# Windowed attention ahead of two expert layers: the scores of a head pair's groups, moved from zero-padded full tiles to quarters of TensorE

## The chip, the core and the metric

The kernel runs on one core of one Trainium2 chip. The metric is the device time of one execution in microseconds (us), lower is better. The engines in the text: PE is TensorE (PEld its weight loads), ACT is ScalarE, DVE is VectorE, POOL is GpSimd, SP is SyncE, which here only starts DMAs.

## What is computed

Three stages follow each other. Attention: 4 batches, 8 heads, 576 positions, head size 64, each query sees the last 64 positions. Then a mixture of 8 experts, each token to one expert, then a dense layer with a clipped quadratic activation. All in fp32. The change touches attention and the way its result X is handed on:

```python
scores = scale * np.matmul(q, k.transpose(0, 1, 3, 2))
rel = pos[:, None] - pos[None, :]
scores = np.where((rel >= 0) & (rel < 64), scores, -1e9)
attn = softmax(scores)
x = np.matmul(attn, v)                     # (B, H, S, D)
x = x.transpose(0, 2, 1, 3).reshape(2304, 512)
logits = x @ w_gate + modality_bias[modality_id]   # argmax picks the expert
out[mask] = gate_w[mask] * (relu(x[mask] @ w1[e]) @ w2[e])
...
return g(out @ w_in) @ w_out
```

## The kernel before

The 2304 tokens are 36 groups of 64 queries, 9 groups to a batch. A group of queries meets 128 keys: the 64 before it and its own (the first group of a batch takes the first 128 keys and another mask). A loop over steps g = 0 to 39 is written as a software pipeline, and each engine runs its instructions in the order in which they are written. In step g:

- `scores(g + 1)`: four matmuls write the bank `sc`, one for each head pair hp. Heads are laid out as par = 0 or 1 on partitions 0 to 63 or 64 to 127, four hp each. The stationary operand is the query tile `Q[:, g, hp]`, 128 partitions by 128 columns, in which each head's 64 queries stand on its own 64 partitions and the rest is zero; so 128 rows of scores come out, 64 for each head of the pair. DVE scales and masks the bank into `sm` (L467) and reduces its maximum to `nm` (L470).
- `turn(g - 1)`: four transposes of the exponentials into `pt`. `weigh(g - 2)`: eight matmuls, each on 64 columns of the array, from `et` and the values V into `o`. In even steps `gates` transposes the X of two groups (one tile of 128 tokens) into `xp`. Every fourth step has the gate's `lp`, every fourth `L` (four small passes of 8 columns).
- On ACT `expo(g)`, four exponentials that take `nm` as bias and sum into `su`; `turned(g - 1)`, the copy of `pt` to `et`; in even steps `gated`, two copies of `xp` halves to `xt`.
- On DVE `norm(g - 1)` and `weighed(g - 2)`, which writes X; then two DMAs on SP store X of the group, one for each par, to `xs` in DRAM.

A block j of three groups is loaded by SP at the start of step 3(j - 2): `load_q` with two DMAs (one for each par, 256 bytes at a time into the zero-padded tile, of which there are three, cleared once by DVE), K with one, V with one. Blocks 0 and 1 are loaded in smaller pieces at the start. SP starts its DMAs strictly in program order, and each waits until the eighth before it has landed.

Behind attention run pieces of the routing (`route`): for each chunk of 4 tiles some 25 small DVE operations, spread over the steps by `between` and `advance`, with a store of `gate` to `xs` (L690). From about step 23 on SP also loads the first expert's eight weight pieces (L241), and POOL splits six of them into a high and a low part (L915, L916); between the third and the fourth POOL starts the gather of block 0's rows from `xs` (L256). Before step 32's scores stand 7 matmuls of `keep` that only pass time; the scores of group 33 behind them are the first that need block 11. PSUM has 7 banks in rotation for all of this.

Of the kernel before, what the change touches and what calls it, by code (L numbers as in the profile page):

```python
# [85 lines left out]
def moe_kernel(tc, qh, kh, vh, wgh, mod, mbias, wall, winh, wouth, out):  # L86
    nc = tc.nc
    with ExitStack() as ctx:
# [26 lines left out]
        mask = [kp.tile([P, P], F32, name=f"mask{i}") for i in range(2)]  # L115
        for i in range(2):
            nc.gpsimd.memset(mask[i], 0.0)
            for par in range(2):
                m = mask[i][par * 64:(par + 1) * 64, :]
                if i == 0:  # L120
# [283 lines left out]
        with tc.tile_pool(name="ap", bufs=2, side="right", reuse_waits="tile") as ap, tc.tile_pool(name="rp", bufs=2, side="right", reuse_waits="tile") as rp:  # L404
            NQ = 3
            qz = [ap.tile([P, 3, 4, 2, 64], F32, name=f"qz{i}", bufs=1) for i in range(NQ)]
            for i in range(NQ):
                for par in range(2):
                    nc.vector.memset(qz[i][64 * par:64 * par + 64, :, :, 1 - par], 0.0)
# [3 lines left out]
            def load(j, then=None):  # L413
# [45 lines left out]

            def scores(g):  # L460
                b, gi, s = win(g)
                Q, K = st["Q", g // 3], st["K", b]
                sc = bank("sc", (P, 4, P))
# [3 lines left out]
                nc.vector.scalar_tensor_tensor(out=sm, in0=sc, scalar=0.125, in1=mask[gi == 0].unsqueeze(1).to_broadcast([P, 4, P]), op0=ALU.mult, op1=ALU.add)  # L467
# [31 lines left out]
            def weigh(g):  # L499
                b, gi, s = win(g)  # L500
                V = st["V", b * 3 + s // 3]
                et = st.pop(("t", g))
                o = bank("o", (P, 4, 64))
# [6 lines left out]
            def weighed(g):  # L510
                o, rc = st.pop(("o", g)), st.pop(("r", g))
                if g % 2 == 0:
                    st["x", g // 2] = ap.tile([P, 2, 4, 64], F32, name="X", bufs=3)
                X = st["x", g // 2]
                nc.vector.tensor_mul(X[:, g % 2], o, rc.unsqueeze(2).to_broadcast([P, 4, 64]))
                for par in range(2):
                    sl = slice(par * 64, par * 64 + 64)
                    nc.sync.dma_start(xs[g * 64:g * 64 + 64, par * 256:par * 256 + 256], X[sl, g % 2].rearrange("p h d -> p (h d)"))

            def gates(t):  # L520
                X = st.pop(("x", t))
                xp = bank("xp", (P, 2, 2, 2, 64))
                for gi in range(2):
                    for i in range(2):
                        nc.tensor.transpose(xp[:, gi, i].rearrange("p a b -> p (a b)"), X[:, gi, 2 * i:2 * i + 2].rearrange("p a b -> p (a b)"), ident)
                st["xp", t] = xp

            def gated(t):
                xp = st.pop(("xp", t))
                if t % 2 == 0:  # L530
                    st["xt"] = ap.tile([P, 2, 2, 2, 2, 64], F32, name="xt", bufs=1)
                for gi in range(2):
                    nc.scalar.copy(st["xt"][:, :, :, t % 2, gi], xp[:, gi])

            def logits(t):
# [3 lines left out]
                for j in range(4):  # L539
                    nc.tensor.matmul(lp[32 * j:32 * j + 32], wgs[:, j], xt[:, j % 2, j // 2].rearrange("p t a b -> p (t a b)"), start=True, stop=True)  # L540
                st["lp"] = lp

            def logits1(t):
                st["lx"] = st["xt"][:, 0, 0].rearrange("p t a b -> p (t a b)")
# [1255 lines left out]
```

## Time and profile before

| | us |
|---|---|
| median of 3 runs (lowest, highest) | 802.19 (800.89, 805.43) |
| the profiled execution | 807.45 |
| its span in the profile | 805.7 |
| PE busy (share of the span) | 763.7 (95%) |
| PEld busy | 658.4 (82%) |
| DVE busy | 505.9 (63%) |
| ACT busy | 350.0 (43%) |
| POOL busy | 301.1 (37%) |

The shares are means over the whole span. Attention takes about the first 125 us of it, and there the shares are others; the rows below are from that stretch. "Clock" is the share of full speed that was granted to TensorE: 1.00 is 2.4 GHz, 0.50 is 1.2 GHz. An fp32 matmul shows as two passes, each with a weight load and a matmul, so four matmuls are eight such pairs.

### The profile page before, as it was taken

What the parts mean: (1) busy time and instruction counts of PE and PEld (TensorE: products, weight loads), DVE (VectorE), ACT (ScalarE), POOL (GpSimd) and SP (SyncE); (2) the same over time, 40 slices, a digit from 0 to 9 for tenths busy, and PEclk for the clock granted to TensorE, in tenths of its full rate; (3) what the DMA queues carried; (4) which work ended last, traced back from release to release, by engine and by line L of the source; (5) the groups of instructions that cost most, each with busy time, mean ns of one, the idle gap of its engine ahead of it and who ended that gap; (6) DMA issues with size and microseconds to landing.
All of it is one profiled execution on the core that took longest, in us unless ns stands there. A gap on an engine that the chain in (4) does not pass through costs nothing. (4 is left out here: it accounts for less than half of the span.)

```text
span 805.7 us, 14482 instructions
## 1 busy us (share of the span) xinstructions
PE 763.7 (95%) x4935; PEld 658.4 (82%) x4935; DVE 505.9 (63%) x1012; ACT 350.0 (43%) x827; POOL 301.1 (37%) x257
## 2 busy tenths in 40 slices
PE   6999979999999999989799899999989999999996
PEld 5888868999878886868697679999988888888874
DVE  6788886787766466511675556798868356453540
ACT  4899743232233324523353434344445435433440
POOL 5000572124323153201453332335625656475441
PEclk8999979999999999999899999999999999999999
DMA  8888941357887959445574565748845444353411
GB/s 204 236 224 259 287 149 33 112 194 244 287 282 280 314 197 360 150 148 170 147 235 156 183 211 164 214 156 267 281 173 150 120 135 117 104 143 107 130 46 39
DMA packets 101014, 149.21 MB, mean 185 GB/s; under 512 B 30096, under 2 KB 65456, under 8 KB 100928
## 3 DMA queue, kind: packets, MB, share of 16 engines
q1 hardware_dynamic: 95664, 132.30, 52.4%
q0 software_dynamic: 4736, 15.61, 6.2%
q8 instruction: 41, 0.67, 0.3%
q14 instruction: 45, 0.37, 0.1%
q10 hardware_dynamic: 528, 0.26, 0.1%
HBM read 132.00 MB, written 45.50 MB: 220 GB/s over the span
## 5 line engine op out<-in xcount | busy, mean ns | idle before, releaser
L1610 POOL TENSOR_TENSOR AR<-RA,AR 128x768 fp32r<-128x768 f32 x43 | 81.8, 1923 | 44.0 <-ACT AR L1609 43.9
L82 POOL TENSOR_TENSOR cv_g<-cv_g,cv_a 128x512 f32<-128x512 f32 x32 | 45.2, 1426 | 128.3 <-DVE cv_a L80 82.8
L1724 PE MATMUL ob<-WG,AR 128*128 128x512 f32 x234 | 91.9, 393 | 0.8 <-POOL AR L1610 0.4
L1722 PE MATMUL ob<-WG,AR 128*128 128x512 f32 x234 | 91.5, 391 | 0.0
L1723 PE MATMUL ob<-WG,AR 128*128 128x512 f32 x234 | 91.2, 390 | 0.0
L380 PE MATMUL hp<-xh,AR 128*128 128x256 f32 x512 | 71.1, 280 | 0.0
L380 PEld LDWEIGHTS hp<-xh,AR 128*128 128x128 f32 x512 | 64.6, 188 | 4.7 <-issue 3.4
L1601 DVE TENSOR_SCALAR small<-RA 128x768 f32<-128x768 f32 x48 | 43.7, 912 | 37.7 <-DMA RA<-gs 37.7
L1602 ACT ACTIVATE small<-small,half 128x768 f32<-128x768 f32 x48 | 45.0, 939 | 41.5 <-DVE small L1601 41.5
L477 ACT ACTIVATE ex<-sm,nm 128x128 f32<-128x128 f32 x144 | 56.1, 395 | 14.2 <-DVE nm L470 13.9
L1470 PE MATMUL mz<-AR,WG 128*128 128x384 f32 (+2 forms) x258 | 54.9, 348 | 6.8 <-ACT AR L1202 1.9
L1608 DVE TENSOR_TENSOR RA<-small,RA 128x768 f32<-128x768 f32 x48 | 56.0, 1166 | 7.2 <-ACT small L1602 6.0
L1470 PE MATMUL mv<-AR,WG 128*128 128x384 f32 (+2 forms) x258 | 54.8, 348 | 3.3 <-ACT wide L1510 2.2
L389 DVE SCALAR_TENSOR_TENSOR hl<-hp,hh 128x512 fp32r<-128x512 f32 x32 | 21.9, 690 | 57.2 <-ACT hh L388 35.3
L1470 PEld LDWEIGHTS mz<-AR,WG 128*128 128x128 f32 x258 | 46.3, 194 | 9.6 <-DVE small L1503 2.4
L1724 PEld LDWEIGHTS ob<-WG,AR 128*128 128x128 f32 x234 | 43.9, 188 | 12.3 <-POOL AR L1610 2.9
L1609 ACT CAST AR<-RA 128x768 fp32r<-128x768 f32 x48 | 39.9, 831 | 32.3 <-PE ob L1723 16.2
L398 PE MATMUL yp<-AR,hh 128*128 128x512 f32 x128 | 52.3, 409 | 0.6 <-ACTq L351 0.6
L1470 PE MATMUL mx<-AR,WG 128*128 128x384 f32 x252 | 51.5, 342 | 0.9 <-ACTq L1147 0.8
L1723 PEld LDWEIGHTS ob<-WG,AR 128*128 128x128 f32 x234 | 43.9, 188 | 9.5
L1722 PEld LDWEIGHTS ob<-WG,AR 128*128 128x128 f32 x234 | 44.0, 188 | 9.1
L400 PE MATMUL yp<-AR,hl 128*128 128x512 f32 x128 | 50.6, 395 | 0.0
(395 smaller groups left out, 1738.7 us busy)
## 6 DMA issues: line engine op xcount, KB each, us to landing
WR<-in_wall_dram SPq DMA_DIRECT2D x80, 256.0 KB
RA<-in_wall_dram SPq DMA_DIRECT2D x36, 512.0 KB
raw<-in_wall_dram SPq DMA_DIRECT2D x36, 512.0 KB
RA<-gs SPq DMA_DIRECT2D x48, 384.0 KB
gs<-small SPq DMA_DIRECT2D x51, 192.0 KB
cv_r<-in_winh_dram SPq DMA_DIRECT2D x16, 512.0 KB
gs<-wide SPq DMA_DIRECT2D x36, 192.0 KB
V<-in_vh_dram SPq DMA_DIRECT2D x7, 768.0 KB
```

Of the source, the lines that this page charges most:

```text
L82: nc.gpsimd.tensor_add(z, z, x)
L380: nc.tensor.matmul(o, a, c, start=n == 0, stop=n == 11)
L398: nc.tensor.matmul(yp, h, wh, start=f == 0, stop=False)
L400: nc.tensor.matmul(yp, l, wh, start=False, stop=f == 7)
L477: nc.scalar.activation(ex[:, hp], sm[:, hp], AF.Exp, bias=nm[:, hp:hp + 1], scale=1.0, accum_out=su[:, hp:hp + 1])
L1470: nc.tensor.matmul(out, a, b, start=first and n == 0, stop=n == 5, skip_group_check=not first or part is not ALLT)
L1602: nc.scalar.activation(GQ[n % 4], GQ[n % 4], AF.Square, scale=0.5, bias=half[:, 0:1])
L1608: nc.vector.tensor_max(GT[n % 5], GQ[n % 4], GT[n % 5])
L1610: eng.tensor_sub(l, GT[n % 5], h)
L1722: nc.tensor.matmul(obs[i], h[:, sl], wh, start=f == j == 0, stop=False)
L1723: nc.tensor.matmul(obs[i], h[:, sl], wl, start=False, stop=False)
L1724: nc.tensor.matmul(obs[i], l[:, sl], wh, start=False, stop=f == 7 and j == 1)
```

## The change

Two groups, 2t and 2t + 1, are now taken together. `products(t)` issues 16 matmuls: for each hp and each of the two groups and each par, 64 partitions of queries by 64 columns against 128 keys. Each uses one quarter of the array (its rows by par, its columns by group), and the two par write two banks. What was "the work of group g" in all later functions is now the work of par = g % 2 of both groups. Sizes and counts of `sm`, `nm`, the exponentials, `et` and `o` stay as they were. `products` is issued in the odd steps only, for two groups at once, so the scores of an odd group come one step earlier in PE's order than before.

Q is loaded without zeros: one DMA of 128 partitions for a block, and the six clears by DVE go. X of a tile is stored by one DMA of 128 tokens in place of four. `gated` is one copy in place of two. There are three masks (a third for a pair whose second group opens a batch). The first loads are cut otherwise: queries of groups 0 and 1 in one DMA, then V, K, queries of group 2.

```diff
-            qz = [ap.tile([P, 3, 4, 2, 64], F32, name=f"qz{i}", bufs=1) for i in range(NQ)]
-            for i in range(NQ):
-                for par in range(2):
-                    nc.vector.memset(qz[i][64 * par:64 * par + 64, :, :, 1 - par], 0.0)
+            qz = [ap.tile([P, 3, 4, 64], F32, name=f"qz{i}", bufs=1) for i in range(NQ)]
...
-                    for par in range(2):
-                        nc.sync.dma_start(Q[par * 64:par * 64 + 64, g0:g1, :, par],
-                                          qh[par * 64:par * 64 + 64, (3 * j + g0) * 256:(3 * j + g1) * 256].rearrange("p (g h q) -> p g h q", g=g1 - g0, h=4))
+                    nc.sync.dma_start(Q[:, g0:g1].rearrange("p g h q -> p (g h q)"), qh[:, (3 * j + g0) * 256:(3 * j + g1) * 256])
...
                     load_k(nc.scalar, 0, 128)
-                    load_q(0, 1)
-                    load_q(1, 3)
+                    load_q(0, 2)
+                    load_v(0, 1)
                     load_k(nc.sync, 128, 192)
-                    load_v(0, 1)
+                    load_q(2, 3)
...
+            def products(t):
+                sc = [bank("sc", (P, 4, P)) for par in range(2)]
+                for hp in range(4):
+                    for gi in range(2):
+                        g = 2 * t + gi
+                        b, _, s = win(g)
+                        for par in range(2):
+                            sl = slice(par * 64, par * 64 + 64)
+                            nc.tensor.matmul(sc[par][gi * 64:gi * 64 + 64, hp], st["Q", g // 3][sl, g % 3, hp], st["K", b][sl, hp, s * 64:s * 64 + 128], start=True, stop=True)
+                for par in range(2):
+                    st["sc", 2 * t + par] = sc[par]
+
             def scores(g):
-                for hp in range(4):
-                    nc.tensor.matmul(sc[:, hp], Q[:, gi % 3, hp].rearrange("p a b -> p (a b)"), K[:, hp, s * 64:s * 64 + 128], start=True, stop=True)
+                if g % 2 == 0:
+                    products(g // 2)
+                sc = st.pop(("sc", g))
...
                 for hp in range(4):
-                    for par in range(2):
+                    for gi in range(2):
...
                         nc.tensor.matmul(o[sl, hp], et[:, hp, sl], V[:, s % 3, hp * P + par * 64:hp * P + par * 64 + 64], start=True, stop=True)
...
-                for par in range(2):
-                    sl = slice(par * 64, par * 64 + 64)
-                    nc.sync.dma_start(xs[g * 64:g * 64 + 64, par * 256:par * 256 + 256], X[sl, g % 2].rearrange("p h d -> p (h d)"))
+                if par:
+                    nc.sync.dma_start(xs[t * P:t * P + P, 0:D], X.rearrange("p a h d -> p (a h d)"))
...
-                for gi in range(2):
-                    nc.scalar.copy(st["xt"][:, :, :, t % 2, gi], xp[:, gi])
+                nc.scalar.copy(st["xt"][:, :, t % 2], xp)
```

How the instructions stand now shows best on two engines. On PE, in the middle of attention, this is the order before (line, operation, tiles, size and count; `sc` are scores, `pt` the transposed exponentials, `o` the weighed values):

```order
L465 MATMUL sc<-K,qz_220 128x128 x4
L491 MATMUL pt<-ident,ex 128x128 x4
L507 MATMUL o<-V,et 64x64 x8
L465 MATMUL sc<-K,qz_220 128x128 x4
L491 MATMUL pt<-ident,ex 128x128 x4
L525 MATMUL xp<-ident,X 128x128 x4
L507 MATMUL o<-V,et 64x64 x8
```

And this is the same place of the changed kernel:

```order
L466 MATMUL sc<-K,qz_234 64x128 x16
L501 MATMUL pt<-ident,ex 128x128 x4
L518 MATMUL o<-V,et 64x64 x8
L501 MATMUL pt<-ident,ex 128x128 x4
L535 MATMUL xp<-ident,X 128x128 x4
L518 MATMUL o<-V,et 64x64 x8
```

Eight score matmuls in two batches of four have become sixteen smaller ones in one batch ahead of two steps' other work.

On SP, one block's loads and the X stores around them, before:

```order
L422 DMA qz_221<-in_qh_dram 64x12x64 x2
L426 DMA K<-in_kh_dram 128x4x192
L433 DMA V<-in_vh_dram 128x3x512
L518 DMA xs<-X 64x256 x6
L422 DMA qz_222<-in_qh_dram 64x12x64 x2
```

And in the changed kernel, two blocks long, since a tile's store falls now once, now twice to a block:

```order
L419 DMA qz_235<-in_qh_dram 128x768
L422 DMA K<-in_kh_dram 128x4x192
L429 DMA V<-in_vh_dram 128x3x512
L529 DMA xs<-X 128x512 x2
L419 DMA qz_236<-in_qh_dram 128x768
L422 DMA K<-in_kh_dram 128x4x192
L429 DMA V<-in_vh_dram 128x2x512
L699 DMA xs<-gate 128x4x16
L529 DMA xs<-X 128x512
```

Ten DMAs to a block have become four or five.

On PE around the 7 passing matmuls (`warm`), before; the scores that are the first to read block 11 stand right behind them:

```order
L465 MATMUL sc_1737<-K_1193,qz1_221 128x128 x4
L491 MATMUL pt_1747<-ident_76,ex_1652 128x128 x4
L540 MATMUL lp_1752<-xt_1634,wgs_103 32x256 x4
L507 MATMUL o_1757<-V_1194,et_1731 64x64 x8
...
L857 MATMUL warm_1798<-ident_76 128x128 x7
L465 MATMUL sc_1806<-K_1193,qz2_222 128x128 x4
```

And now, where the first matmul that reads block 11's queries (`qz2`) is the third row:

```order
L466 MATMUL sc_1801<-K_1240,qz1_235 64x128
L466 MATMUL sc_1802<-K_1240,qz1_235 64x128
L466 MATMUL sc_1801<-K_1240,qz2_236 64x128
...
L501 MATMUL pt_1824<-ident_76,ex_1725 128x128 x4
L549 MATMUL lp_1829<-xt_1695,wgs_117 32x256 x4
L518 MATMUL o_1834<-V_1241,et_1796 64x64 x8
...
L866 MATMUL warm_1874<-ident_76 128x128 x7
```

The first use of block 11 has moved from behind the passing matmuls to a place ahead of them, one step earlier.

## Rows read from the trace of the kernel before

**Rows 1.** Busy time by window: from:to, length, engines (instructions), clock, DMA share, GB/s.

```profile
16.00:21.60 5.60, 5.21 (x34) 4.79 (x35) 2.06 (x5) 2.23 (x9) 0.64 (x2) 0.50 1.03 224
24.00:80.00 56.00, 55.66 (x710) 48.42 (x709) 46.60 (x152) 51.50 (x218) 0.00 (x0) 1.00 0.86 238
...
106.40:112.20 5.80, 0.22 (x3) 0.00 (x1) 5.80 (x9) 2.12 (x9) 5.64 (x5) 0.84 0.28 99
112.20:123.40 11.20, 11.20 (x84) 8.89 (x85) 6.38 (x26) 6.26 (x19) 4.99 (x6) 0.50 0.36 89
```

**Rows 2.** Timeline of PE's weight loads, steps 7 to 11: start, length, instructions, [idle before].

```profile
30.26 0.55 PEld L507 LDWEIGHTS o<-V,et 128*64 128x64 f32 x16 [0.41 <-DVE sm L467]
30.87 0.97 PEld L465 LDWEIGHTS sc<-K,qz 128*128 128x128 f32 x8
31.76 0.47 PEld L491 LDWEIGHTS pt<-ident,ex 128*128 128x128 f32 x4
...
32.20 0.53 PEld L554 LDWEIGHTS L<-selg,xt 128*128 128x128 f32 x4
...
40.09 0.16 PEld L540 LDWEIGHTS lp<-xt,wgs 128*32 128x32 f32 x8 [0.17 <-ACT ex L477]
40.66 0.43 PEld L507 LDWEIGHTS o<-V,et 128*64 128x64 f32 x12 [0.41 <-issue]
```

**Rows 3.** Timeline of ACT, the copies of an even step.

```profile
38.05 0.56 ACT L496 COPY et<-pt 128x512 f32<-128x512 f32 x1
38.52 0.63 ACT L533 COPY xt<-xp 128x256 f32<-128x256 f32 x2
```

**Rows 4.** Waits of DVE, 24 to 80 us: total us, times, longest.

```profile
DVE sm L467 <- PE sc L465: 7.4, 16, 0.7
```

**Rows 5.** Timeline of the start: scores of group 4, and ACT around them.

```profile
11.11 0.56 ACT L496 COPY et<-pt 128x512 f32<-128x512 f32 x1
...
14.75 0.40 ACT L477 ACTIVATE ex<-sm,nm 128x128 f32<-128x128 f32 x1
...
16.39 2.04 PE L465 MATMUL sc<-K,qz 128*128 128x128 f32 x8 [3.52 <-DMA qz<-in_qh_dram]
...
19.92 0.40 ACT L477 ACTIVATE ex<-sm,nm 128x128 f32<-128x128 f32 x1
...
23.52 0.42 ACT L477 ACTIVATE ex<-sm,nm 128x128 f32<-128x128 f32 x1
```

**Rows 6.** Timeline of SP, which starts the DMAs: start, length of the issues.

```profile
65.84 3.73 SPq L518 DMA_DIRECT2D xs<-X  x6
70.32 1.34 SPq L422 DMA_DIRECT2D qz<-in_qh_dram  x2
...
72.45 0.45 SPq L433 DMA_DIRECT2D V<-in_vh_dram  x1
...
93.48 0.63 SPq L426 DMA_DIRECT2D K<-in_kh_dram  x1
```

**Rows 7.** Timeline of the end of attention, all engines.

```profile
73.91 0.40 ACT L477 ACTIVATE ex<-sm,nm 128x128 f32<-128x128 f32 x1
...
82.36 0.40 ACT L477 ACTIVATE ex<-sm,nm 128x128 f32<-128x128 f32 x1
...
93.64 0.97 PEld L465 LDWEIGHTS sc<-K,qz 128*128 128x128 f32 x8
...
99.72 1.13 PE L465 MATMUL sc<-K,qz 128*128 128x128 f32 x8 [1.18 <-DMA K<-in_kh_dram]
...
102.23 1.05 POOL L256 DMA_INDIRECT xg<-xs,idi  x1 [6.59 <-PE xp L525]
...
108.00 2.31 DVE L678 SCALAR_TENSOR_TENSOR rt<-jt,rank 128x4 f32<-128x4 f32 x1
...
112.20 0.29 PEld L525 LDWEIGHTS xp<-ident,X 128*128 128x128 f32 x2 [5.82 <-DVE X L515]
...
130.63 0.16 DVE L678 SCALAR_TENSOR_TENSOR rt<-jt,rank 128x4 f32<-128x4 f32 x1
```

More of the change, by code (lines that the diff above doesn't have):

```diff
@@ L114, in moe_kernel @@
         make_identity(nc, ident)
-        mask = [kp.tile([P, P], F32, name=f"mask{i}") for i in range(2)]
-        for i in range(2):
+        mask = [kp.tile([P, P], F32, name=f"mask{i}") for i in range(3)]
+        for i in range(3):
             nc.gpsimd.memset(mask[i], 0.0)
@@ L119, in moe_kernel @@
                 m = mask[i][par * 64:(par + 1) * 64, :]
-                if i == 0:
+                if i != par + 1:
                     nc.gpsimd.affine_select(out=m, in_=m, pattern=[[-1, P]], compare_op=ALU.is_ge, fill=-1e9, base=64, channel_multiplier=1)
@@ L458, in win @@
                 return b, gi, s
-            def scores(g):
-                b, gi, s = win(g)
-                Q, K = st["Q", g // 3], st["K", b]
-                sc = bank("sc", (P, 4, P))
-                for hp in range(4):
-                    nc.tensor.matmul(sc[:, hp], Q[:, gi % 3, hp].rearrange("p a b -> p (a b)"), K[:, hp, s * 64:s * 64 + 128], start=True, stop=True)
+            def products(t):
[9 more added lines that the diff above has]
+                    st["sc", 2 * t + par] = sc[par]
+            def scores(g):
+                if g % 2 == 0:
+                    products(g // 2)
+                sc = st.pop(("sc", g))
+                firsts = [win(g // 2 * 2 + gi)[1] == 0 for gi in range(2)]
                 sm = sms[g % 4]
-                nc.vector.scalar_tensor_tensor(out=sm, in0=sc, scalar=0.125, in1=mask[gi == 0].unsqueeze(1).to_broadcast([P, 4, P]), op0=ALU.mult, op1=ALU.add)
+                nc.vector.scalar_tensor_tensor(out=sm, in0=sc, scalar=0.125, in1=mask[1 if firsts[0] else 2 if firsts[1] else 0].unsqueeze(1).to_broadcast([P, 4, P]), op0=ALU.mult, op1=ALU.add)
                 between(0, g)
@@ L511, in weighed @@
                 o, rc = st.pop(("o", g)), st.pop(("r", g))
[L512 to L515, printed above, removed]
-                for par in range(2):
-                    sl = slice(par * 64, par * 64 + 64)
-                    nc.sync.dma_start(xs[g * 64:g * 64 + 64, par * 256:par * 256 + 256], X[sl, g % 2].rearrange("p h d -> p (h d)"))
-            def gates(t):
-                X = st.pop(("x", t))
-                xp = bank("xp", (P, 2, 2, 2, 64))
-                for gi in range(2):
-                    for i in range(2):
-                        nc.tensor.transpose(xp[:, gi, i].rearrange("p a b -> p (a b)"), X[:, gi, 2 * i:2 * i + 2].rearrange("p a b -> p (a b)"), ident)
+                t, par = divmod(g, 2)
+                if par == 0:
+                    st["x", t] = ap.tile([P, 2, 4, 64], F32, name="X", bufs=3)
+                X = st["x", t]
+                nc.vector.tensor_mul(X[:, par], o, rc.unsqueeze(2).to_broadcast([P, 4, 64]))
+                if par:
+                    nc.sync.dma_start(xs[t * P:t * P + P, 0:D], X.rearrange("p a h d -> p (a h d)"))
+            def gates(t):
+                X = st.pop(("x", t)).rearrange("p a h d -> p (a h d)")
+                xp = bank("xp", (P, 4, P))
+                for j in range(4):
+                    nc.tensor.transpose(xp[:, j], X[:, j * P:j * P + P], ident)
                 st["xp", t] = xp
@@ L530, in gated @@
                 if t % 2 == 0:
-                    st["xt"] = ap.tile([P, 2, 2, 2, 2, 64], F32, name="xt", bufs=1)
-                for gi in range(2):
-                    nc.scalar.copy(st["xt"][:, :, :, t % 2, gi], xp[:, gi])
+                    st["xt"] = ap.tile([P, 4, 2, P], F32, name="xt", bufs=1)
+                nc.scalar.copy(st["xt"][:, :, t % 2], xp)
             def logits(t):
@@ L539, in logits @@
                 for j in range(4):
-                    nc.tensor.matmul(lp[32 * j:32 * j + 32], wgs[:, j], xt[:, j % 2, j // 2].rearrange("p t a b -> p (t a b)"), start=True, stop=True)
+                    nc.tensor.matmul(lp[32 * j:32 * j + 32], wgs[:, j], xt[:, j].rearrange("p t a -> p (t a)"), start=True, stop=True)
                 st["lp"] = lp
             def logits1(t):
-                st["lx"] = st["xt"][:, 0, 0].rearrange("p t a b -> p (t a b)")
+                st["lx"] = st["xt"][:, 0].rearrange("p t a -> p (t a)")
                 nc.scalar.copy(st["lx"], st.pop("lp"))
```

6 lines of the change are left out of this document (4 added, 2 removed).

## Prediction

> **What bounds the kernel now.** Only attention, the first 125 us, is changed; all behind it keeps its instructions, so I read that stretch alone and count what it gives up as what the kernel gives up. First the busy time by window. From 24 to 80 us PE is busy 55.66 of 56 us at full clock, ACT 51.50, DVE 46.60 [rows 1]. PE is the bound there, but ACT is close behind. The waits say the same: DVE's most common wait is for `sc` from PE, 7.4 us in 16 times [rows 4]. The clock of the pipeline I read from ACT, whose exponentials of group g open step g: group 5 at 23.52, group 24 at 73.91, so 50.39 / 19 = 2.65 us to a step [rows 5, 7].
>
> Then the two places where PE is not busy. At the start the scores of group 4 wait 3.52 us for their queries, and PE then runs at half clock from 16 to 21.6 us [rows 1, 5]. At the end, PE idles 5.82 us up to 112.20, waiting for an X from DVE, while DVE and POOL are both busy nearly all of that window (5.80 and 5.64 of 5.80 us), and then works at half clock until 123.4 [rows 1, 7]. The DVE time there is not work: one operation on 4 columns takes 2.31 us at 108.00 and 0.16 us at 130.63, when POOL is still [rows 7]. POOL's weight splits hold DVE up.
>
> **The change part by part.**
>
> *The middle, steps 5 to 24.* Price of the scores now: 8 pairs of weight load and matmul from 30.87 to 31.76, 0.89 us, or 0.111 each; four steps run from `o` at 30.26 to `o` at 40.66, 10.40 us, and hold four such batches, 3.56 us [rows 2]. What replaces two of them is 32 pairs on quarters. No row shows a quarter. The nearest below is `lp`, quarter columns, 8 loads in 0.16 us, 0.020 a pair; the nearest above is `sc` itself, 0.111, if quarters did not run beside each other. Much nearer than both is `o`: it loads the same 64 columns, on two halves in turn, 16 pairs from 30.26 to 30.87, 0.61 us, 0.038 a pair [rows 2]. I take that one, since its weight loads have the size of the new ones and the load is what a pair waits for: `L`, whose matmuls move only 8 columns, takes 0.53 us for 4 loads, no less a pair than `sc` with 128 [rows 2]. A change between full and part columns shows as 0.17 us idle ahead of `lp` [rows 2]; `products` adds one. So 32 x 0.038 + 0.17 = 1.39 us for two groups in place of 1.78. Four steps then take PE 10.40 - 3.56 + 2.78 = 9.62, or 2.40 a step; with 0.020 a pair 2.12, with 0.111 it would be 3.57.
>
> ACT comes next. The window holds 56 / 2.65 = 21.1 steps, so ACT works 51.50 / 21.1 = 2.44 us a step, DVE 46.60 / 21.1 = 2.21 [rows 1]. One copy of 512 columns takes 0.56, the two of 256 take 0.63 [rows 3], so the merged copy saves ACT 0.07 in two steps: 2.40. PE and ACT would then both need 2.40 and DVE 2.21. Three engines that wait for each other are never all full, so I take 2.45 a step: (2.65 - 2.45) x 19 = 3.8 us. Upper end 2.40: 4.8 us. Lower end nothing, if the waits between engines over 90% busy eat it; below nothing only by the quarter price, a rival below.
>
> *The start.* Group 4's queries belong to a load that wrote 256 bytes at a time, behind two DMA starts for each load. It becomes one DMA of whole rows. If they come in time, ACT sets the pace: its exponentials of group 3 start their last at 14.75 and one copy of 0.56 follows, so group 4's can start at about 16.0 in place of 19.92 [rows 3, 5]: 3.9 us. Group 5's came 3.60 later, through the half clock; at 2.45 that is 1.15 more. Together 5.0. Upper end: the wait of 3.52 and half of the 4.79 us of weight loads in the slow window [rows 1, 5], 5.9. Against it stands that `products` of groups 2 and 3 now stand ahead of `turn(0)` and need a K piece and block 1's queries; but the copy that takes `turn(0)`'s result began only at 11.11 [rows 5], behind two groups of exponentials, so some 2 us of that are covered. If the loads are bound by bytes and not by their many short pieces, little comes in earlier: lower end 1. DVE's six clears and POOL's one extra mask lie beside the first loads and cost nothing; were the mask late, DVE's first operation would be, by under 1.5 us.
>
> *SP's queue.* Six X stores take SP 3.73 us, two query loads 1.34, K 0.63, V 0.45 [rows 6]: 6.15 of the 8 us that three steps last, with the waits for earlier DMAs on top. SP runs late by this: block 11's loads stand ahead of step 27 (its exponentials start at 82.36), but its K is issued at 93.48 [rows 6, 7]. With 128-partition stores and loads priced like V, a block takes 1.5 x 0.45 + 0.45 + 0.63 + 0.45 = 2.2 us. This is not on the path by itself; it moves what hangs on SP.
>
> *The end, from step 24.* What hangs there: K of block 11 (scores waited 1.18 us for it at 99.72), and the gather at 102.23, for which POOL sat 6.59 us [rows 7]. A profile names PE for that wait, but the gather reads `xs`, and the last of the stores it needs, the second `gate`, stands on SP behind block 11's loads. Behind the gather POOL splits three more pieces, and these are what DVE runs into from 103 to 114. With SP on time the gather and the splits come some 10 us earlier relative to the steps, before the long routing operations of the third chunk. What could come back: 5.82 of idle PE, 8.89 / 2 = 4.4 of half clock, 1.2 of the K wait, 11.4 us [rows 1, 7]. But splits must run somewhere, and wherever DVE meets one it pays up to 2.31 - 0.16 = 2.15 us [rows 7]; three of them could cost 6.5. I take 5.0, a bit under half, with ends -2 and 11.4.
>
> Sum: 3.8 + 5.0 + 5.0 = 13.8 us. Against the profiled execution that is 807.45 - 13.8 = 793.7. That execution lies 5.3 us above the median; I assume the difference stays and forecast 802.19 - 13.8 = 788.4.
>
> **The rivals.**
>
> *ACT and DVE hold the pace.* PE gets lighter, and the step stays near 2.60 since ACT waits for `nm` and DVE for `sc` in turn: the middle gives 1, the end nothing as DVE is full there, the start its 5.0. Sum 6: 796. For it: ACT's 51.50 of 56 us [rows 1]. Against it: DVE's 7.4 us of waits for `sc` [rows 4] go with the shorter scores. The Trainium skill (TensorEngine Tiling (Array Packing), Performance Considerations, PSUM Bottleneck) says that tiling speeds up TensorE but not the emptying of PSUM, which can become the bound; the trace agrees so far that ACT has under a tenth of the window free.
>
> *The whole end comes back.* Middle and start as in the forecast, the end 11.4: 20.2, some 782; with upper ends everywhere 780.
>
> *Block 11 is late where it is now needed.* Scores of group 33 move one step ahead, to where 93.64 stood; if K still lands at 99.7, PE stops for 6.1 us with nothing to cover it, and half clock costs another 4.4 [rows 1, 7]: 10.5 against 8.8 gained, 804. It decides if SP's queue and the DMAs stay as late as now in spite of half as many starts.
>
> *Quarters do not run beside each other.* Then 32 pairs cost 0.111 each, a step 3.57 on PE, 0.9 us more over some 30 steps: 27 lost, 5 gained, 824. It decides from 0.050 a pair, (1.78 - 0.17) / 32. Against it: the halves of `o` and the quarter columns of `lp` do run beside each other [rows 2]. For it: no row splits the array by rows.
>
> **How the numbers follow.** Chances: forecast 0.50, whole end 0.15, ACT and DVE 0.17, block 11 late 0.10, quarters in turn 0.05, others 0.03. The predicted time is that of the first, 788.4. The range runs from 780 (all upper ends) to 802 (start 1, middle and end about nothing); left out are the last three and a sliver, under 2 in 10. About 0.5%, 4.0 us, is what a measurement of this kernel can tell from no change. Under 798.2 lie the forecast, the whole end and nearly all of the ACT and DVE case: 0.80. Within lie block 11 and a part of the rest: 0.13. Slower: 0.07.
>
> **What the profile after would show.** Right if: 32 score loads take near 1.2 us; exponentials of group 4 start near 16, steps 5 to 24 are near 2.45 apart with ACT above 95% busy; SP has pauses; the gather starts within four steps of step 27; no PE idle of 5 us and no half clock before 120. Wrong if: scores still wait for queries at the start; the 32 loads take over 1.6 us; PE stops in step 31; DVE is held as long as before, only elsewhere.

## The result, and the profile after

| | before | after |
|---|---|---|
| median of 6 runs (lowest, highest), us | 802.89 (800.85, 805.43) | 796.50 (794.20, 798.73) |
| the profiled execution, us | 807.45 | 794.20 |
| measured again: median (number of runs), us | 805.02 (23) | 794.85 (6) |

The ratio of the first comparison is 0.9905 (95%: 0.9884 to 0.9927), of the second 0.9883 (0.9850 to 0.9916). By medians the change gives 6.4 and 10.2 us; the forecast was 788.4, 14 us less than before. The two profiled executions differ by 13.25. Of all the executions below, two of `b_piece`'s ten, its profiled one (814.2 us) among them, ran over 1.5% above their kernel's fastest and are left out of its median and ratio.

First the pace of the pipeline, on ACT's timeline of after (start, length, instruction): groups 4, 5, 24, 27 and 35, which answer to [rows 5, 7].

```profile
16.55 0.40 ACT L487 ACTIVATE ex<-sm,nm 128x128 f32<-128x128 f32 x1 [0.30 <-DVE nm L480]
...
19.04 0.40 ACT L487 ACTIVATE ex<-sm,nm 128x128 f32<-128x128 f32 x1
...
64.77 0.40 ACT L487 ACTIVATE ex<-sm,nm 128x128 f32<-128x128 f32 x1
...
75.60 0.40 ACT L487 ACTIVATE ex<-sm,nm 128x128 f32<-128x128 f32 x1 [1.38 <-DVE nm L480]
...
105.19 0.40 ACT L487 ACTIVATE ex<-sm,nm 128x128 f32<-128x128 f32 x1
```

Group 5 is 4.48 us earlier than before and group 24 is 9.14 us earlier, so the middle gave 4.66: (64.77 - 19.04) / 19 = 2.41 us a step instead of 2.65. The common mark behind attention is the first matmul of the gathered block's second layer, `yp`, on PE's timeline, before and after:

```profile
135.43 2.11 PE L305 MATMUL yp<-AR,h0h 128*128 128x512 f32 x8
```

```profile
121.61 2.11 PE L306 MATMUL yp<-AR,h0h 128*128 128x512 f32 x8
```

13.82 us earlier, so the end from group 24 on gave another 4.68. Now the busy time by window (columns as in [rows 1]):

```profile
16.00:21.60 5.60, 5.18 (x93) 4.00 (x87) 5.15 (x15) 5.30 (x23) 1.24 (x3) 1.00 0.84 297
24.00:64.00 40.00, 37.99 (x683) 29.23 (x680) 35.83 (x119) 38.92 (x164) 0.00 (x0) 1.00 0.87 276
24.00:80.00 56.00, 50.95 (x880) 39.86 (x878) 51.39 (x159) 51.16 (x214) 10.35 (x6) 0.97 0.89 291
96.00:112.00 16.00, 14.56 (x196) 11.44 (x195) 13.38 (x57) 12.33 (x40) 4.06 (x6) 0.98 0.22 69
112.20:123.40 11.20, 11.07 (x83) 9.29 (x82) 9.99 (x35) 3.46 (x8) 3.75 (x2) 1.00 0.20 50
```

The half clock of 112 to 123 is gone. From 24 to 64 ACT is busy 97% and DVE 90%; from 64 to 80 POOL comes in, and PE is idle for 3 us more than in the same time before. What is late there is X from DVE (waits of PEld, 24 to 80 us: total, times, longest; the longest ends at 72.9, and the granted clock is at its half level from about 73 to 76), while DVE's wait for scores, 7.4 us in [rows 4], has shrunk:

```profile
PEld xp L535 <- DVE X L527: 6.2, 5, 3.3
...
DVE sm L477 <- PE sc L466: 3.0, 7, 0.6
```

The price of the scores, on the timeline of PE's weight loads: 32 loads in 0.86 us, and 1.04 until PE's next group starts. That is 0.86 / 32 = 0.027 a pair, so four pairs on quarters take about the time of one full pair before, 0.111.

```profile
27.64 0.86 PEld L466 LDWEIGHTS sc<-K,qz 64*64 64x64 f32 x32
28.68 0.42 PEld L501 LDWEIGHTS pt<-ident,ex 128*128 128x128 f32 x4 [0.17 <-ACT xt L542]
```

SP is no longer behind: one block's loads and a store, each a single short issue. In the last row K of block 11 is issued before group 27's exponentials (75.60) start; in the kernel before it came 11 us behind them [rows 6, 7].

```profile
55.85 0.34 SPq L529 DMA_DIRECT2D xs<-X  x1
56.28 0.38 SPq L419 DMA_DIRECT2D qz<-in_qh_dram  x1
56.72 0.44 SPq L422 DMA_DIRECT2D K<-in_kh_dram  x1
57.25 0.61 SPq L429 DMA_DIRECT2D V<-in_vh_dram  x1
...
74.89 0.43 SPq L422 DMA_DIRECT2D K<-in_kh_dram  x1
```

So POOL starts its splits earlier, at 67.48 us instead of 81.47, and there DVE runs into them. POOL, then DVE, of after:

```profile
68.60 2.35 POOL L925 TENSOR_TENSOR AR<-RA,AR 128x1024 fp32r<-128x1024 f32 x1
...
84.97 1.05 POOL L257 DMA_INDIRECT xg<-xs,idi  x1 [5.03 <-DMA raw<-in_wall_dram]
...
90.58 2.34 POOL L925 TENSOR_TENSOR AR<-raw,AR 128x1024 fp32r<-128x1024 f32 x1
92.86 1.04 POOL L924 CAST AR<-raw 128x1024 fp32r<-128x1024 f32 x1
93.98 2.35 POOL L925 TENSOR_TENSOR AR<-raw,AR 128x1024 fp32r<-128x1024 f32 x1
96.27 0.54 POOL L770 MEMSET xg<- 128x528 f32 x1
```

```profile
69.28 1.84 DVE L683 SCALAR_TENSOR_TENSOR cols<-iota_j,jt,tk 128x144 fp32r<-128x144 f32 x1
...
90.66 2.31 DVE L634 TENSOR_TENSOR pg<-lg,mx 128x32 f32<-128x32 f32 x1
92.89 0.41 DVE L527 TENSOR_TENSOR X<-o,rc 128x256 f32<-128x256 f32 x1
93.22 0.67 DVE L477 SCALAR_TENSOR_TENSOR sm<-sc,mask 128x512 f32<-128x512 f32 x1
93.93 0.69 DVE L480 TENSOR_REDUCE nm<-sm 128x4 f32<-128x512 f32 x1
94.54 2.30 DVE L491 TENSOR_SCALAR rc<-su 128x4 f32<-128x4 f32 x1
```

An operation of 32 columns (90.66) takes 2.31 us, as long as POOL's subtraction runs, and ends with it. One of four columns (94.54) takes 2.30 us and outlasts the subtraction: it ends at 96.84, with the clear behind it. X and the scaled scores, which read PSUM, take their usual time beside a cast, and the maximum (a reduction) beside a subtraction. Over their undisturbed times the nine held operations from 67 to 97 us lose 13.4 us, and one more loses 4.4 at 111. In the trace before the sum is 13.1, all of it from 84 to 128. In this pair of profiles the change has not shortened the holds; it has moved them ahead.

### The profile page after: what moved, and what is told of

The parts are those of the page before. It is cut to its first block, busy times and chain, and to the rows that moved or that the text cites. A ratio compares the mean times of both kernels' runs of the same rounds, so it can differ in the third digit from the quotient of the medians.

```text
span 792.3 us, 14927 instructions
## 1 busy us (share of the span) xinstructions
PE 747.6 (94%) x5223; PEld 637.7 (80%) x5223; DVE 503.7 (64%) x1006; ACT 347.5 (44%) x809; POOL 302.6 (38%) x262
## 5 line engine op out<-in xcount | busy, mean ns | idle before, releaser
L381 PE MATMUL hp<-xh,AR 128*128 128x256 f32 x512 | 71.1, 280 | 0.0
L1610 DVE TENSOR_SCALAR small<-RA 128x768 f32<-128x768 f32 x48 | 45.4, 947 | 39.3 <-DMA RA<-gs 39.3
L381 PEld LDWEIGHTS hp<-xh,AR 128*128 128x128 f32 x512 | 64.6, 188 | 4.7 <-issue 3.4
```

What stands on the lines that cost most here:

```text
L381: nc.tensor.matmul(o, a, c, start=n == 0, stop=n == 11)
L1610: nc.vector.tensor_scalar(GQ[n % 4], GT[n % 5], -1.0, 1.0, ALU.max, ALU.min)
```

## The experiments

All times are medians; "before" ran beside them with 805.0, 805.7, 805.3 and 804.7 us in the four later measurements. The marks are read as above.

| kernel | us (lowest, highest) | ratio to before (95%) | group 5 | group 24 | group 35 | yp |
|---|---|---|---|---|---|---|
| before, first profile | 802.9 (800.9, 805.4) | | 23.52 | 73.91 | 115.21 | 135.43 |
| b_again | 806.2 (800.8, 809.7) | 1.0008 (0.9980, 1.0036) | 22.05 | 74.37 | 120.06 | 137.45 |
| after, first profile | 796.5 (794.2, 798.7) | 0.9905 (0.9884, 0.9927) | 19.04 | 64.77 | 105.19 | 121.61 |
| a_again | 794.9 (790.7, 797.5) | 0.9883 (0.9850, 0.9916) | 18.07 | 63.78 | 106.53 | 122.95 |
| a_q256 | 803.7 (801.1, 807.0) | 0.9983 (0.9960, 1.0006) | 21.26 | 70.13 | 111.13 | 128.00 |
| a_x4 | 798.1 (796.3, 799.0) | 0.9915 (0.9885, 0.9944) | 17.97 | 67.22 | 108.21 | 125.83 |
| a_half | 808.5 (803.8, 815.3) | 1.0062 (1.0025, 1.0100) | 19.03 | 72.94 | 118.80 | 135.20 |
| a_piece | 792.8 (790.0, 794.9) | 0.9863 (0.9809, 0.9917) | 18.64 | 64.38 | 101.81 | 122.08 |
| b_piece | 807.6 (801.2, 812.4) | 1.0029 (0.9990, 1.0069) | 21.95 | 72.35 | 119.97 | 140.17 |
| a_dvesub | 796.4 (792.4, 799.9) | 0.9905 (0.9872, 0.9938) | 18.38 | 64.12 | 108.58 | 128.38 |
| a_rc | 795.3 (793.5, 799.1) | 0.9864 (0.9822, 0.9905) | 18.16 | 63.84 | 104.95 | 122.61 |
| a_rcp | 791.3 (786.3, 795.4) | 0.9807 (0.9755, 0.9858) | 18.07 | 63.74 | 105.54 | 122.96 |
| a_rcpk | 788.8 (783.9, 795.2) | 0.9790 (0.9733, 0.9847) | 18.83 | 64.50 | 106.81 | 123.23 |
| a_pace | 791.2 (790.7, 793.9) | 0.9832 (0.9792, 0.9872) | 18.79 | 64.46 | 96.38 | 119.66 |

**Both kernels again.** No edit.

> The kernel before, unchanged, for a second profile and more times. Its first profile (807.45 us) lies 4.6 us above the median of its six timed runs (802.89), and the changed kernel's (794.20) 2.3 below its own (796.50); the two profiles differ by 13.25 us, the medians by 6.4. Theory 1: what varies is the end of attention (the idle of 5.82 us up to 112.20 and the half clock behind it), so the end term of the sum was read from an untypical execution: a profile of about 803 has its first expert matmul (hp) at 137 to 139 instead of 141.95. Rival: what varies lies behind attention: hp starts at 141 to 142 again, whatever the time of the execution.

> The changed kernel, unchanged, second profile. Theory 1 (the end of attention varies): hp starts within 1 us of 128.12 only if the time is near 794, and 2 to 3 us later at 796.5. Rival (behind attention): hp starts at 127.6 to 128.6 whatever the time. Median 796.5, ratio to before 0.99, by either.

The second pair of profiles gives 14.50 us at `yp`; the two executions of one kernel lie 2.0 and 1.3 us apart there. So attention's gain in the profiles repeats. The `hp` of the two expectations (the first weight load of L380, of L381 after the change) stands at 143.97 and 129.46, outside the ranges of theory and rival in both. The theory that the end varied downwards from 141.95 is not borne out: the second profile of before has the same stop, longer (PE timeline), with a clock of 0.61 from 110 to 120.

```profile
117.05 0.69 PE L525 MATMUL xp<-ident,X 128*128 128x128 f32 x2 [7.00 <-DVE X L515]
```

But both profiled executions of before (807.45, 807.53) lie 2.4 above the mean of all 87 runs of before, 805.1, and both of after (794.20, 790.69) 1.3 and 4.8 below the mean of its twelve, 795.5. The runs of either kernel scatter about their mean by some 2.4 us (standard deviation), so that an execution 2.4 off is no rarity. By means the change gives 9.6 us, by the profiles 15.0. From `yp` to the end of the span, where the two kernels have the same instructions, before takes 670.3 and 668.4, after 670.7 and 665.9, and the other kernels made from after between 666.5 and 675.6: that part varies by more than 5 us and is not longer after the change. The profiles do not say where the ordinary execution of before is faster than the two seen.

**The query loads undone.**

```diff
-            qz = [ap.tile([P, 3, 4, 64], F32, name=f"qz{i}", bufs=1) for i in range(NQ)]
+            qz = [ap.tile([P, 3, 4, 2, 64], F32, name=f"qz{i}", bufs=1) for i in range(NQ)]
...
-                    nc.sync.dma_start(Q[:, g0:g1].rearrange("p g h q -> p (g h q)"), qh[:, (3 * j + g0) * 256:(3 * j + g1) * 256])
+                    for par in range(2):
+                        nc.sync.dma_start(Q[par * 64:par * 64 + 64, g0:g1, :, par],
+                                          qh[par * 64:par * 64 + 64, (3 * j + g0) * 256:(3 * j + g1) * 256].rearrange("p (g h q) -> p g h q", g=g1 - g0, h=4))
...
-                            nc.tensor.matmul(..., st["Q", g // 3][sl, g % 3, hp], ...)
+                            nc.tensor.matmul(..., st["Q", g // 3][sl, g % 3, hp, par], ...)
```

> The changed kernel with the query loads alone undone: two DMAs to a load again, 256 bytes at a time into a tile with gaps (the gaps are not used and not cleared). Theory: the start's gain (exponentials of group 5 at 19.04 instead of 23.52) comes from the whole-row loads; they return to 23 to 24, the time rises by 4 to 5 us over the changed kernel, to 801. Rival: the short pieces never bound the start, the order of the first loads and the freed DVE did it: group 5 within 1 us of 19.0 and the time within 1 us of 796.5.

803.7, 8.2 over the mean of after: nearly the whole gain is gone, more than expected, and not where expected. Of the start's gain 2.2 us are lost against the first profile of after, 3.2 against the second (group 5 at 21.26). Against the two profiles of before 0.8 to 2.3 us stay, so the form of the loads need not be all of the start's gain. The middle then goes at (70.13 - 21.26) / 19 = 2.57, although its PE work is that of after. The loads crowd out each other: the second batch of scores waits for K, in the middle SP spends 3.05 us on one block's queries and K, where after spends 0.82, and from 24 to 64 us the DMA engines are busy for 0.99 of the time and move 261 GB/s, where in after it is 0.87 and 276 (PE, then SP, then the window).

```profile
10.74 1.97 PE L468 MATMUL sc<-K,qz 64*64 64x128 f32 x28 [2.40 <-DMA K<-in_kh_dram]
```

```profile
56.62 1.46 SPq L420 DMA_DIRECT2D qz<-in_qh_dram  x2
58.13 1.59 SPq L424 DMA_DIRECT2D K<-in_kh_dram  x1
```

```profile
24.00:64.00 40.00, 35.65 (x642) 27.78 (x643) 32.51 (x105) 36.70 (x151) 0.00 (x0) 1.00 0.99 261
```

The whole-row query load is the part of the change without which the rest is worth little: the ratio to before, 0.9960 to 1.0006, includes no change at all. What the whole rows would give without the quarters was not run.

**The X stores undone.**

```diff
-                if par:
-                    nc.sync.dma_start(xs[t * P:t * P + P, 0:D], X.rearrange("p a h d -> p (a h d)"))
+                for gi in range(2):
+                    sl = slice(gi * 64, gi * 64 + 64)
+                    nc.sync.dma_start(xs[t * P + gi * 64:t * P + gi * 64 + 64, par * 256:par * 256 + 256], X[sl, par].rearrange("p h d -> p (h d)"))
```

> The changed kernel with the X stores alone undone: four DMAs of 64 rows by 1 KB to a tile instead of one. Theory: SP's late queue is what the end of attention hangs on; block 11's K and the gather (84.97) come some 8 us later, the first split (67.48) too, and the time rises by 3 to 5 us, to 800. Rival: an earlier gather and earlier splits only move DVE's hold-ups to other operations; the time stays within 1 us of 796.5, or falls.

2.6 us over the mean of after, just under the lower end expected; `yp` comes 2.9 to 4.2 later. The first split starts at 72.21 instead of 67.48, the gather at 90.31 instead of 84.97, 5 us later and not 8. SP's queue is worth some 3 us of the gain, most of them already before group 24 (67.22), where a batch of scores waits 1.00 us for K at 53 us and the granted clock is at its half level from about 52 to 56.

**More PE work in the scores.**

```diff
-                            nc.tensor.matmul(sc[par][gi * 64:gi * 64 + 64, hp], ...)
+                            for _ in range(2 - par):
+                                nc.tensor.matmul(sc[par][gi * 64:gi * 64 + 64, hp], ...)
```

> The changed kernel with every score matmul of par 0 issued twice: 16 more pairs of weight load and matmul to two steps, at 0.027 us each 0.43, or 0.22 us a step more on PE; nothing else changes. Theory: ACT alone holds the pace of the middle (it has no idle time in steps 8 to 16, which are 2.32 us apart), PE has room: steps 5 to 24 stay within 0.05 us of 2.41 and the time within 1.5 us of the changed kernel. Rival (the prediction's floors, PE and ACT both at 2.40): PE goes to 2.6 a step, the middle loses 4 us, the time rises by 4 to 7 us.

13 us over after. The dose was not what I had set: the timeline of weight loads shows 48 loads in 1.78 us.

```profile
69.38 1.78 PEld L467 LDWEIGHTS sc<-K,qz 64*64 64x64 f32 x48
```

16 more pairs cost 0.92 us, 0.057 each, not 0.027: each stands right behind a pair on its own quarter, and this reads as such a pair getting no cover from it. So PE got 0.46 us a step more, and the pace went from 2.41 to (72.94 - 19.03) / 19 = 2.84, by 0.43. PE's work in after is 10.40 - 3.56 + 2 x 1.04 = 8.92 us to four steps, 2.23 a step (working of the prediction with the measured price); with 0.46 it is 2.69, and PE is the bound. "ACT alone, PE has room" can be said of no more than about 0.2 us a step. At this dose, the only one run, nearly all that PE was given more came out as pace.

**POOL's splits in pieces**, in after and in before.

```diff
-                        (nc.scalar.copy if split0 in ACTS else nc.gpsimd.tensor_copy)(WH[split0], raws[0][split0])
-                        nc.gpsimd.tensor_sub(WL[split0], raws[0][split0], WH[split0])
+                        if split0 in ACTS:
+                            nc.scalar.copy(WH[split0], raws[0][split0])
+                        for q in range(0, 1024, 256):
+                            if split0 not in ACTS:
+                                nc.gpsimd.tensor_copy(WH[split0][:, q:q + 256], raws[0][split0][:, q:q + 256])
+                        for q in range(0, 1024, 256):
+                            nc.gpsimd.tensor_sub(WL[split0][:, q:q + 256], raws[0][split0][:, q:q + 256], WH[split0][:, q:q + 256])
```

> The changed kernel with POOL's weight splits cut: each cast and each subtraction of 1024 columns becomes four of 256. Same work, same place in the order. Theory: in the end of attention DVE's small operations are held until POOL's running instruction ends (up to 2.31 us; from 67 to 97 us the held ones lose about 13 us in all), and that is what keeps the end from coming back; with pieces of 0.6 us the holds shrink, the first expert matmul (hp) comes 4 to 8 us earlier than 128 to 129 and the time falls by 4 to 8 us. Rival: DVE loses against POOL as a whole, not by the instruction; it is held as long in more and shorter waits, and the time stays within 1.5 us.

> The kernel before with POOL's weight splits cut in the same way. Theory: the idle of 5.8 us of PE near 110 and the half clock behind it come from the same holds, so they go and the time falls by 4 to 8 us from 805; the change's gain in the end is then mostly a matter of which DVE operations the splits meet. Rival: within 1.5 us of before, the end there is held by SP's late loads and by PE.

The time of a_piece, 792.8 from four runs, is 2.7 under the mean of after, less than the theory's 4 to 8, and the intervals of the two overlap. Its held operations take at most 1.1 us up to group 35, and group 32 starts at 89.49 instead of 94.65. Then one stop of PE, and behind it half clock for 12 us (PE timeline, then the window):

```profile
98.79 0.69 PE L535 MATMUL xp<-ident,X 128*128 128x128 f32 x2 [3.45 <-DVE X L527]
```

```profile
99.00:111.00 12.00, 12.00 (x90) 9.16 (x91) 5.50 (x27) 6.79 (x17) 4.17 (x6) 0.52 0.31 93
```

`yp` is where it was, 122.08. In after the stop of 4.12 us stands ahead of `keep`'s passing matmuls, which ran at the slow clock in place of useful ones: 14 loads in 3.06 us. Why the clock was back after 3 us there and after some 11.5 us in a_piece, the runs do not show.

```profile
93.36 3.06 PEld L866 LDWEIGHTS warm<-ident 128*128 128x128 f32 x14 [4.12 <-DVE X L527]
```

b_piece gained nothing (807.6, a ratio that includes 1). Its profile, of an execution 6.6 us above that median, has one operation of DVE held for 11.37 us, through all POOL instructions from 103.5 to 114.6, and a stop of PE of 11.35 us.

```profile
103.46 11.37 DVE L674 SCALAR_TENSOR_TENSOR cols<-iota_j,jt,tk 128x144 fp32r<-128x144 f32 x1
```

So the theory of single instructions is half right: DVE gets in between two of POOL's instructions often, but not always.

**The subtractions on DVE.**

```diff
-                        nc.gpsimd.tensor_sub(WL[split0], raws[0][split0], WH[split0])
+                        (nc.gpsimd if split0 in ACTS else nc.vector).tensor_sub(WL[split0], raws[0][split0], WH[split0])
```

> The changed kernel with the six subtractions of the splits moved from POOL to DVE, the casts stay on POOL. Theory: DVE pays some 1.1 us for each, 6.6 in all, in place of some 13 us of holds; hp comes 3 to 5 us earlier and the time falls by 3 to 5 us. Rival: DVE is the bound of the end and the casts of 1.04 us go on holding it, so 6.6 us of work on the path take the place of the holds: no change, or up to 3 us slower.

No gain (796.4), as the rival had it, but by another way: DVE now waits in order for POOL's cast, which stands behind the gather (DVE).

```profile
87.31 3.01 DVE L925 TENSOR_TENSOR AR<-RA,AR 128x1024 fp32r<-128x1024 f32 x1 [4.71 <-POOL AR L924]
```

**Without the addition; with pieces; with cover for PE.**

```diff
-                nc.vector.tensor_scalar_add(rc, st.pop(("s", g))[3], 1e-9)
                 between(2, g)
-                nc.vector.reciprocal(rc, rc)
+                nc.vector.reciprocal(rc, st.pop(("s", g))[3])
```

a_rcp adds the edit of a_piece; a_rcpk also this:

```diff
+                    late = 24 <= g < G and g % 2 == 0
-                    if g >= 4 and g % 2 == 0:
+                    if g >= 4 and g % 2 == 0 and not late:
                         gates((g - 4) // 2)
...
                         weigh(g - 2)
+                    if late:
+                        keep(4)
+                        gates((g - 4) // 2)
```

> The changed kernel without the addition of 1e-9 to the sum of the exponentials (L491): each sum is at least 1, so in fp32 the addition leaves the value as it is; the reciprocal takes the sum itself. One DVE operation on 4 columns less in each step, but it is one of those that POOL holds, and X waits behind it (in the two profiles of the changed kernel it was held for 1.74, 1.03, 2.30 and for 1.03, 2.30 us). Theory: the end is bound by DVE's queue with the holds in it; without this operation 3 to 5 us of holds go, the time falls by 2 to 5 us. Rival: a hold passes to the next routing operation in the queue; the time stays within 1.5 us of the changed kernel (795.5).

> a_rc and a_piece together (no addition, POOL's splits in pieces of 256 columns). a_piece had its exponentials of group 32 at 89.5 instead of 94.7 to 96.0 us, but one PE idle of 3.45 us at 98.8 and half clock from 99.4 to 110.9 gave it back. Theory: holds shrink again, fewer idles of PE over 3 us: time 3 to 7 us under the changed kernel, to 790. Rival: POOL holds DVE over trains of its instructions (11.4 us in b_piece), pieces make that no better, and the half clock comes back: within 1.5 us of a_piece (792.8).

> a_rcp, and in the even steps from 24 to 34 PE does the weighing (o) and four passing matmuls of 0.06 us a pass before the transposes that wait for X, so that it idles less in one piece. Theory: what a_piece lost, it lost to the half clock that follows an idle of PE over 3 us; with the cover there is none from 70 to 115 us, the yp matmuls start at 115 to 118 instead of 121.6 to 123, and the time is 4 to 8 us under the changed kernel, to 789. Rival: the passing matmuls lie on PE's path, 0.5 us in each of six steps, and cost what the clock gives: within 1.5 us of a_rcp.

a_rc is as fast as after: the hold passes to the next operation in the queue (an operation of the routing, 2.23 us at 67.62). With pieces, group 32 comes 7 to 11 us earlier than in the two profiles of after (85.21 in a_rcp and 87.76 in a_rcpk, against 94.65 and 96.00), and then both profiles show one long hold, in a_rcp of 10.96 and in a_rcpk of 9.56 us, through some twenty instructions of POOL up to its last (DVE, then POOL, of a_rcpk):

```profile
89.92 9.56 DVE L674 TENSOR_SCALAR jt<-rank 128x4 f32<-128x4 f32 x1
```

```profile
90.23 1.42 POOL L931 CAST AR<-raw 128x256 fp32r<-128x256 f32 x4
91.63 2.77 POOL L933 TENSOR_TENSOR AR<-raw,AR 128x256 fp32r<-128x256 f32 x4
94.35 1.42 POOL L931 CAST AR<-raw 128x256 fp32r<-128x256 f32 x4
95.74 2.76 POOL L933 TENSOR_TENSOR AR<-raw,AR 128x256 fp32r<-128x256 f32 x4
98.45 1.01 POOL L769 MEMSET xg<- 128x528 f32 x2
```

Even so a_rcpk is the fastest kernel of the study by its median, 788.8, with runs from 783.9 to 795.2, though its interval overlaps that of a_rcp. Each four passing matmuls took PE 0.97 us, twice what was expected. Its `yp` in the profile, 123.23, is not the 115 to 118 expected: PE stops for 5.99 us, up to 100.89, cover or not. Whether the long hold is what spreads its times over 11 us is not shown: there is one trace of each kernel.

**POOL paced by DVE.** The edit of a_rc, and:

```diff
-                for w in behind[:1]:
-                    if w.pe is None:
-                        w.step()
+                for n in range(1 if g < 23 or g >= G else 4 if i == 2 else 0):
+                    for w in behind[:1]:
+                        if w.pe is None:
+                            w.step()
...
-            ACTS = (6, 7)
+            ACTS = (5, 6, 7)
+            HALF = {25: [(0, 0)], 26: [(0, 1)], 27: [(1, 0)], 28: [(1, 1)], 31: [(2, 0)], 32: [(2, 1)], 33: [(3, 0)], 34: [(3, 1)], 35: [(4, 0), (4, 1)]}
...
+                    for c, z in HALF.get(g, ()):
+                        z = slice(512 * z, 512 * z + 512)
+                        nc.gpsimd.tensor_copy(pace, st["r", g - 1][:, 0:1])
+                        nc.gpsimd.tensor_copy(WH[c][:, z], raws[0][c][:, z])
+                        nc.gpsimd.tensor_sub(WL[c][:, z], raws[0][c][:, z], WH[c][:, z])
+                        split0 = c + 1
```

with the order of a_rcpk on PE, two passing matmuls in place of four, and the last three splits whole from step 35 on.

> a_rc, and POOL paced by DVE: from step 25 each half of a split (512 columns of cast and subtraction) begins with a one-column copy of the reciprocals (rc) of that step, so POOL works while DVE does X, the scaled scores and their maximum, which were not held beside POOL in any trace so far, and stands still while DVE does routing operations, which were; the routing operations of a step stand together ahead of the reciprocal (from step 23 to 35), the weighing stands ahead of X's transposes with two passing matmuls, the third to sixth piece come some steps later, and the sixth is cast by ACT. No work less than in a_rc. Theory: the holds are what the end loses; with them gone steps 25 to 35 come at 2.3 to 2.9 us instead of 3.7 (exponentials of group 35 at 91 to 97 instead of 105 to 106.5), yp starts at 112 to 117 instead of 121.6 to 123, the time is 5 to 9 us under the changed kernel (786 to 791). Rival: without the holds something else sets the end (the first gather, the weight pieces for the first expert, which now come later, or PE itself): yp within 2 us of 122, time within 1.5 us of a_rc.

Up to group 35 it does what the theory says: 96.38 instead of 105 to 107, no stop of PE over 0.7 us from 62 to 96, no hold over 1 us. POOL waits for DVE's reciprocal, works 2.1 us and waits again:

```profile
73.72 0.19 POOL L931 COPY pace<-rc 128x1 f32<-128x1 f32 x1 [1.14 <-DVE rc L492]
73.84 0.62 POOL L932 CAST AR<-RA 128x512 fp32r<-128x512 f32 x1
74.54 1.27 POOL L933 TENSOR_TENSOR AR<-RA,AR 128x512 fp32r<-128x512 f32 x1
77.02 0.19 POOL L931 COPY pace<-rc 128x1 f32<-128x1 f32 x1 [1.21 <-DVE rc L492]
```

Of the 8.6 to 10.2 us that it is ahead at group 35, 2 to 3 are left at `yp` (119.66): behind it stand a stretch at half clock (granted 0.66 from 100 to 110) and the last two splits, which POOL ends at 116.2. The time is 791.2, 4.3 under the mean of after; its six runs lie within 3.2 us, where a_rcpk's spread over 11.3. Both expectations were half right: with the holds gone groups 24 to 35 come (96.38 - 64.46) / 11 = 2.90 us apart instead of 3.67, and behind them the splits and PE set the end. Both a_rcpk and a_pace are faster than before and than the mean of after. Beside the pacing a_pace has the routing operations together, later splits, one more cast on ACT and PE's order changed; how much each of these does was not separated.

## Why the prediction was right, and which term was mis-sized

**Direction and mechanisms** were right, 796.5 lies within 780 to 802, and so were the three terms against the profiled executions: middle 3.8 forecast, 4.66 measured (the second pair of profiles, whose kernel before lost 1.9 us more in the middle, gives 6.6); start 5.0, measured 4.48 and 3.98; end 5.0, measured 4.68 and 3.91. Sum 13.8, measured 13.82 and 14.50. That the sum fits so closely is partly luck: the misses of the terms cancel, and the end's 5.0 was a choice between -2 and 11.4, not worked out.

**The mis-sized step is the last one:** "That execution lies 5.3 us above the median; I assume the difference stays". It did not. First, more than half of the 5.3 was not the execution's: the median of three, 802.19, lies 2.9 below the mean of the 87 runs of before, and the execution only 2.4 above it. From the mean the same sum gives 805.1 - 13.8 = 791.3, 4.2 under the mean of after. Second, both profiles of before are above its ordinary run and both of after below its own, so 13.8 us taken from one execution became 6.4 and 10.2 in the medians. What the surplus of before consisted of is open. One candidate, argued and not shown, is the stop of 5.8 and 7.0 us at the end with the half clock behind it: the hold that makes it depends on whether DVE gets in between two of POOL's instructions, and a_piece and a_rcp, with the same pieces, differ in that. But they differ in an addition too, and both profiles of before have the stop, so that it comes and goes between executions of one kernel was not seen. Without the end's 5.0 the forecast would have been 793.4.

**The price of a quarter pair**, 0.038, was 0.027: 1.04 us for 32 instead of 1.39. The row of `lp`, 0.020, was nearer than that of `o`. (The reading of `L` beside it took the length of a group; from its start to the next start, as for `sc`, `L` takes 0.09 us a load, less than 0.111.) PE's floor fell to 2.23 instead of 2.40, but ACT's stayed, and the step came to 2.41 and not to 2.23. The Trainium skill (TensorEngine Tiling (Array Packing), Performance Considerations, PSUM Bottleneck) says that the emptying of PSUM may become the bottleneck when tiling speeds up TensorE. ACT's 97% from 24 to 64 us agrees in part: most of ACT's step is four exponentials of data in SBUF, some 0.4 us each, and only its copies empty PSUM.

**The start**: the wait of 3.52 us for group 4's queries is gone, as forecast. Waits of the second batch (groups 2 and 3) took part of its place, 0.66 us for queries and 1.14 for K on PE's timeline of after, and in the first profile the clock was at half from 8 to 14 us:

```profile
6.83 0.43 PE L466 MATMUL sc<-K,qz 64*64 64x128 f32 x4 [0.66 <-DMA qz<-in_qh_dram]
8.41 1.97 PE L466 MATMUL sc<-K,qz 64*64 64x128 f32 x28 [1.14 <-DMA K<-in_kh_dram]
```

That the form of the loads makes about half of the start's gain or more is shown by a_q256. How far it reaches was not foreseen: the same loads also slow the middle, so the parts of the sum were not independent.

**The end**: SP is on time, the gather stands at 84.97, three steps after group 27's exponentials (75.60), block 11 is not waited for. The rule of the wrong-if list, "DVE is held as long as before, only elsewhere", applies: 13.4 us and 4.4 more, before 13.1. That the end returned 4.7 of 11.4 us fits this; how much of the rest the holds make was not measured, but a_pace, with holds of under 1 us, is 8.8 to 10.2 us ahead of after at group 35. "No idle of 5 us" held in the first profile (4.12) and not in the second (5.52); "no half clock before 120" did not hold: in the first profile the clock was at half from 8 to 14, 73 to 76 and 92 to 96 us.

**The rivals**: quarters that don't run beside each other, a late block 11 and the whole end are out. "ACT and DVE hold the pace", 796, gave the right time by the wrong terms: its middle of 1 us was 4.7.

## What to carry to other kernels

A sum made against one profiled execution predicts that execution; before it is set against a median, ask which of its terms are stops that another execution may not have, or profile twice. When DVE's small operations stand in one queue with its critical ones, a second engine's long elementwise work is not out of the way by starting earlier: the holds move with it. Pacing it by the first engine's own progress, with the reordering that went with it, gave a steadier kernel here than cutting it up (six runs within 3.2 us, against 9.1 and 11.3). A change to matmuls can hang on the form of the DMA that feeds them: undoing the query load alone cost 8.2 us of 9.6.

## What the hardware showed that was not expected

- POOL can hold a DVE operation over far more than one of its instructions: 10.96 and 9.56 us behind pieces of 0.35 to 0.7 us, until POOL's last. The Trainium skill (SBUF — State Buffer, Who interferes with whom) says that where DVE and GpSimd both want the ports that they share, the one that issues first has them for its whole instruction and the other blocks; the hold of 2.31 us at 90.66 agrees, the long ones go beyond it. It also says that reductions, and operations with at most one input from SBUF outside DVE's two-port modes, don't meet GpSimd there; the rows of `nm`, `sm` and X agree (0.69 us beside a subtraction, 0.67 and 0.41 beside a cast).
- Pairs on quarters in turn cost 0.027 us, four of them as much as one full pair; an added pair behind one on the same quarter cost 0.057, with the same 64 by 64 load.
- In a_piece a stop of PE of 3.45 us was followed by half clock for 11 to 12 us of busy matmuls; in after a stop of 3.27 us at 72.9 was followed by some 3 us of it, and at 93.4, where seven passing matmuls stood first, they took the slow stretch of 3 us themselves.
